# VectorE's first weight chunk and first v queued behind the first pair's copies, with that pair's k loaded from ScalarE's queue

## The chip, the cores and the metric

The kernel runs on one core of a Trainium2 chip. The metric is the device time of one execution in microseconds (us). The engines work side by side, each through its own instruction list in a fixed order: TensorE (PE, with its weight loads as PEld), VectorE (DVE), ScalarE (ACT), GpSimd (POOL) and SyncE (SP), which here does nothing but start transfers. ScalarE can start transfers too. An instruction that has to wait holds up everything behind it on its engine.

## What is computed

Attention over 4 batches of 8 heads, 576 positions and a head width of 64, in which only scores within tau of the row's maximum are kept; then two expert layers on the 2304 rows that come out.

```python
scores = scale * np.matmul(q, k.transpose(0, 1, 3, 2))
thresh = np.max(scores, axis=-1, keepdims=True) - tau
scores = np.where(scores >= thresh, scores, -1000000000.0)
attn = np.exp(scores - np.max(scores, axis=-1, keepdims=True))
x = np.matmul(attn / (np.sum(attn, axis=-1, keepdims=True) + 1e-09), v)
...
h = x @ w_in                        # first layer, 512 -> 2048
g = (a[0] + a[1]*h + a[2]*h**2 + a[3]*h**3) / (1.0 + abs(b[0])*abs(h) + abs(b[1])*h**2 + 1e-6)
x = g @ w_out                       # 2048 -> 512
...
h = x @ w_in                        # second layer, other weights
g = np.where(h >= 1.0, h, np.where(h <= -1.0, 0.0, (h + 1.0)**2 / 4.0))
out = g @ w_out
```

## The kernel before

All matrix products are made from pairs of 16-bit parts (a value and what is left of it), so every operand is scaled by a power of two and split into `hi` and `lo` first. For q and k that is `prep_pair`, which handles two heads (a pair) at a time: it loads q and k, squares them on ScalarE (L345) to bound them, finds the largest entry over all partitions with two TensorE products and a VectorE maximum (`everywhere`, L188, L189), makes a scale of it (`root`, L169 to L173), and splits (L215 and L216). For the first pair of the first batch, `turned` then transposes q and k with TensorE (L324) and copies the results out of PSUM: q by ScalarE (L328), k by VectorE (L330), and `kT2`, k with its two halves of the partitions exchanged, half by ScalarE (L331) and half by VectorE (L332). The other pairs are transposed by a transfer.

The weights arrive as 64-bit numbers. Each of the two layers has eight chunks, and each chunk two halves (`x` = 0 for w_in, 1 for w_out). `convert` loads a half of 1 MB into a tile `rw`, of which there are two, rebuilds 32-bit numbers in a tile `wt`, of which there are three, with three VectorE instructions (L229, L230, L231), bounds them (TensorE L254, VectorE L255, L189, L169 to L173), scales them on ScalarE (L218) and splits them (ScalarE L209, four GpSimd subtractions L213, which end the use of the `wt` tile). The first layer's halves stay on the chip as `wc`; the second layer's, `wh`, go back to memory.

The first batch's attention is a generator of its own, `first_attention`: pair 0 is prepared, v is loaded in ten pieces and bounded by VectorE (`first_v`, L510 to L522), pair 1 is prepared, and then for each of four pairs `row_max` finds the row maxima of the scores (TensorE L540 and L541, VectorE L544), which go into a row `mrow` (L580), and `transposed`, `sums`, `take` and `divide` do the rest, ending with the tiles `xT` (L633, L634). The next pair's `row_max` runs beside the current pair. After that come steps: 24 per layer and batch (three blocks of 192 rows by eight chunks), each a first product (L863), the function between (L744 to L757 in the first layer, L808 to L810 in the second) and a second product (L877). The attention of the next batch, 36 row tiles called softmax rows below (L442, L444, L404), runs beside those steps.

The order in which each engine gets its instructions is made when the kernel is built, by a scheduler that goes by priorities (`at`): a moved instruction may thus move many others. `tc.issue_after(ins)` makes the instructions of its block that run on the engine of `ins` stand behind `ins` in that engine's list; those on other engines are not bound. SP and ScalarE start transfers in the order of their lists.

Names in the rows: `wt_0_1` is chunk 0, half 1; `mqke` the bound of q and k; `qkr` their scale; `mv` the bound of v; `sm` and `mx` the scores and maxima of `row_max`.

Of the kernel before, what the change touches and what calls it, by code (L numbers as in the profile page):

```python
# [43 lines left out]
def tile_attention_moe_moe2(  # L44
# [18 lines left out]
    V, A, G, T, Q = nc.vector, nc.scalar, nc.gpsimd, nc.tensor, nc.sync  # L63
    B, H, S, D = q.shape
    P = 128
    NP = H // 2
    NT = S // P
    ST = S - NT * P
# [40 lines left out]
    def small(n, name, keep=False):  # L109
        if keep:  # L110
            return cp.tile([P, n], F32, name=name)
        tag = "".join(x for x in name if x.isalpha() or x == "_").rstrip("_")
        return sp.tile([P, n], F32, name=name, tag=f"s{n}_{tag}", bufs=4 if tag in ("mx", "nt") else 2)
# [62 lines left out]
    def at(when):  # L176

        return tc.high_priority(tc.cur_priority - int(1000 * (when + 100)))
# [83 lines left out]
    def make_half(m, i, x, wc, on_vector):  # L262
        convert(m, i, x, wc[:, x * HALF : (x + 1) * HALF], on_vector)
        if x == 1:
            with at(8 + i):
                Q.dma_start(scratch[m][i], wc)
# [20 lines left out]
    def whole(x):  # L287
        return x[..., 0 : NT * P, :].rearrange("h (p t) d -> p h (t d)", t=NT)

    def prep_v(b, on_vector=True):  # L290
# [24 lines left out]
                split(to[:, :, 0:D], to[:, :, D + 1 : 2 * D + 1], raw[:, n0:n1], s_x[b], on_vector)  # L315
        return vv

    def turned(qk, qT, kT, kT2):
        last = ps_1.tile([P, 512], F32, name="qk_t8", tag="ph1")
        for x in (1, 0):  # L320
            most = ps_2.tile([P, 1024], F32, name=f"qk_t{x}", tag="s" if x else "acc")
            for c in range(C):
                dst = most[:, c * P : (c + 1) * P] if c < C - 1 else last[:, x * P : (x + 1) * P]
                T.matmul(dst, qk[:, x, c], ident16, start=True, stop=True)  # L324
            for src, c0, c1 in ((most, 0, C - 1), (last[:, x * P : (x + 1) * P], C - 1, C)):
                src = src.rearrange("p (c s) -> p c s", s=P)
                if x == 0:
                    A.copy(qT[:, c0:c1], src)  # L328
                else:
                    V.tensor_copy(kT[:, c0:c1], src)  # L330
                    A.copy(kT2[0:D, c0:c1], src[D : 2 * D])  # L331
                    V.tensor_copy(kT2[D : 2 * D, c0:c1], src[0:D])  # L332

    def prep_pair(b, pr, on_vector=True):
        raws = rp.tile([P, 2, C + 1, D], F32, name=f"rqk{b}_{pr}", tag="rqk", bufs=1)
        raw = raws[:, :, 0:C, :]
        for x, src in enumerate((q, k)):
            Q.dma_start(raws[:, x].rearrange("p (a c) d -> p a (c d)", a=2)[:, :, 0 : NT * D],
                        whole(src[b, 2 * pr : 2 * pr + 2]))
            for ab in range(2):  # L340
                Q.dma_start(raw[ab * ST : (ab + 1) * ST, x, NT, :], src[b, 2 * pr + ab, NT * P :, :])
        mx = small(2, f"mqk{b}_{pr}")
        qk = ap.tile([P, 2, C, 2 * D], F16, name=f"qk{b}_{pr}", tag="qk", bufs=1)
        for x in range(2):
            A.activation(qk[:, x, :, 0:D], raw[:, x], AF.Square, scale=2.0**-32, accum_out=mx[:, x : x + 1])  # L345
        f = small(2, f"qkf{b}_{pr}")
        s = root(f"qkr{b}_{pr}", f, everywhere(f"mqke{b}_{pr}", mx, 2), 2.0**96, n=2)

        con = sp.tile([P, 4], F32, name=f"con{b}_{pr}", tag="con", bufs=3)
        V.scalar_tensor_tensor(con[:, 0:1], f[:, 0:1], cflag, f[:, 1:2], op0=ALU.mult, op1=ALU.mult)  # L350
        V.tensor_scalar(con[:, 1:2], con[:, 0:1], -1.0, None, op0=ALU.mult)
        V.scalar_tensor_tensor(con[:, 2:3], s[:, 0:1], tau8, s[:, 1:2], op0=ALU.mult, op1=ALU.mult)
        V.tensor_tensor(con[:, 2:3], con[:, 2:3], tlow, op=ALU.min)
        if b == 0:
            V.tensor_scalar(con[:, 3:4], con[:, 2:3], STEEP, -LARGEST, op0=ALU.mult, op1=ALU.max)
        for x in range(2):
            split(qk[:, x, :, 0:D], qk[:, x, :, D : 2 * D], raw[:, x], s[:, x : x + 1], on_vector)
        if b > 0 or pr < 2:
            qkT = ap.tile([P, 2 * C, P], F16, name=f"qkT{b}_{pr}", tag="qkT")
            qT, kT = qkT[:, 0:C], qkT[:, C : 2 * C]  # L360
            kT2 = ap.tile([P, C, P], F16, name=f"kT2{b}_{pr}", tag="kT2")
            if b == 0 and pr == 0:
                turned(qk, qT, kT, kT2)
                return con, qT, kT, kT2
            Q.dma_start_transpose(out=qkT, in_=qk.rearrange("p x c d -> p (x c d)"))
        else:
            qT, kT, kT2 = (ap.tile([P, C, P], F16, name=f"{x}{b}_{pr}", tag="eT" if pr == 2 else "hl", bufs=N_ROW)
                           for x in ("qT", "kT", "kT2"))
            for x, t in enumerate((qT, kT)):
                Q.dma_start_transpose(out=t, in_=qk[:, x].rearrange("p c d -> p (c d)"))  # L370
        Q.dma_start(kT2[0:D], kT[D : 2 * D])
        Q.dma_start(kT2[D : 2 * D], kT[0:D])
        return con, qT, kT, kT2
# [265 lines left out]
    def first_attention():  # L639

        pairs = [prep_pair(0, 0)]
        yield
        vv = first_v()
        xT[0] = [xp.tile([P, 2 * KT, TB], F16, name=f"xT0_{j}", tag="xT", bufs=NB) for j in range(NB)]
        mrows = [xp.tile([P, 1152], F16, name="mrow0", tag="yT", bufs=NB), mp.tile([P, 1152], F16, name="mrow1", tag="yo", bufs=1)]
        for t in mrows:
            G.memset(t, 0.0)
        yield
        pairs.append(prep_pair(0, 1, False))
        yield  # L650
        for _ in row_max(0, *pairs[0][1:], mrows[0]):
            yield
        n = 0
        for pr in range(NP):
            data = *pairs[pr], mrows[pr % 2]
            rows = row_max(pr + 1, *pairs[pr + 1][1:], mrows[(pr + 1) % 2]) if pr + 1 < NP else iter(())
            x = ap.tile([P, S], F32, name=f"x0_{pr}", tag="e", bufs=N_SC)
            d = ap.tile([P, S], F32, name=f"d0_{pr}", tag="sc", bufs=N_SC)
            held = []
            for ab, t in [(0, t) for t in range(NT + 1)] + [(1, t) for t in range(NT)]:  # L660
                e = transposed(pr, ab, t, data, n)
                for f in held:
                    f()
                if t == 0:
                    pv = [ps_1.tile([P, 512], F32, name=f"pv{z}_{pr}_{ab}", tag=tag)[:, 0 : S // 2]
                          for z, tag in enumerate(("pv", "ph1"))]
                    held = [partial(sums, pv, 1, pr, NT, tail, vv, True, False)] if ab else []
                    held.append(partial(sums, pv, ab, pr, t, e, vv, not ab, False))
                elif t == NT or (ab and t == NT - 1):
                    held = [partial(sums, pv, ab, pr, t, e, vv, False, True), partial(take, pv, ab, x, d)]  # L670
                    tail = e
                else:
                    held = [partial(sums, pv, ab, pr, t, e, vv, False, False)]
                for _ in range(2 if n % 9 < 6 else 1):
                    next(rows, None)
                n += 1
                yield
                if n in PREPARE:
                    pairs.append(prep_pair(0, len(pairs), False))
                    yield  # L680
            for f in held:
                f()
            divide(pr, x, d)
        yield
# [164 lines left out]
    chunks = {}  # L849
# [33 lines left out]
    steps = [(n, m, b, j, i) for n, (m, b) in enumerate(phases) for j in range(NB) for i in range(NCH)]  # L883

    att = first_attention()
    halves = [(i, x) for i in range(NCH) for x in range(2)]
    for i in range(NCH):
        chunks[0, i] = new_chunk(0, i)
    for n in range(N_FIRST):
        with at(36 * n / N_FIRST - 40):  # L890
            next(att)
        while halves and len(halves) * N_FIRST > 2 * NCH * (N_FIRST - 1 - n):
            with at(2.4 * (2 * NCH - len(halves)) - 39.5):
                i, x = halves.pop(0)
                make_half(0, i, x, chunks[0, i], False)


    beside = [[] for _ in steps]
# [79 lines left out]
```

## Time and profile before

| | |
|---|---|
| median of 3 runs | 1236.59 us (1235.79 to 1240.24) |
| the profiled execution | 1239.17 us, its span 1237.1 us |
| TensorE matmul / weight load busy | 1095.3 us (89%) / 988.4 us (80%) |
| VectorE busy | 979.3 us (79%) |
| ScalarE / GpSimd busy | 839.5 us (68%) / 542.7 us (44%) |
| moved by transfers | 175.51 MB, mean 142 GB/s |
| mean granted TensorE clock | 0.963 of full speed |

The busy shares are averages over stages with different limits: the start and the first attention, a stage in which the first layer runs beside the conversion of the second layer's weights, and a long stage of steps. The table by stages among the rows below separates them. "Idle before" in a row is the time in which that engine did nothing ahead of the instruction, with what ended it.

### The profile page before, as it was taken

How to read it: one execution, taken by the hardware profiler on the slowest of the kernel's cores; microseconds unless marked ns; L12 is line 12 of the kernel's file. 1: busy time of each engine (PE TensorE's matmuls, PEld its weight loads, DVE VectorE, ACT ScalarE, POOL GpSimd, SP SyncE). 2: the span in 40 equal slices, each digit the busy share in tenths (PEclk: the TensorE clock that was granted, in tenths of full speed). 3: DMA queues.
4: the chain of work that ended last, by engine and by line, in shares of the span. 5: the costliest groups of instructions: out<-in, count | busy, mean ns of one | idle time of the engine just before them, and what ended most of it. 6: DMA issues, size and time to landing. Idle time of an engine off the chain costs nothing.

```text
span 1237.1 us, 31750 instructions
## 1 busy us (share of the span) xinstructions
PE 1095.3 (89%) x12636; PEld 988.4 (80%) x12636; DVE 979.3 (79%) x2362; ACT 839.5 (68%) x1532; POOL 542.7 (44%) x698
## 2 busy tenths in 40 slices
PE   2778788588899999898888998998899999999998
PEld 1445456477888989898778888997888998999997
DVE  8887896999997377799997766899996768896431
ACT  2577777698887377677875766887675667775332
POOL 2445545656666266322564454223563553222221
PEclk9888888899899999999999999999999999999999
DMA  7677576635269158813785639422984467007000
GB/s 220 224 205 252 210 266 238 220 93 137 49 151 249 29 111 185 218 28 90 183 225 95 115 64 250 136 50 68 242 195 71 81 171 221 15 2 261 15 14 27
DMA packets 217845, 175.51 MB, mean 142 GB/s; under 512 B 179680, under 2 KB 190944, under 8 KB 209504
## 3 DMA queue, kind: packets, MB, share of 16 engines
q1 hardware_dynamic: 216464, 171.38, 52.6%
q8 instruction: 99, 1.62, 0.5%
q10 hardware_dynamic: 1232, 2.10, 0.5%
q14 instruction: 50, 0.41, 0.1%
HBM read 106.83 MB, written 21.50 MB: 104 GB/s over the span
## 4 chain that ended last, share of the span: by engine, by line
PE 40%; DVE 24%; DMA 11%; POOL 9%; issue 9%; ACT 6%; SPq 1%; DVEq 0%; ACTq 0%; POOLq 0%
PE acc L877 15%; PE ph L863 15%; DMA eT<-hl 8%; POOL hl L415 3%; PE pv L613 2%; PE pv L430 2%; DVE t L746 2%; POOL wh L213 2%; DVE e L404 2%; DVE t L751 2%; DVE sc L442 2%; POOL gg L213 1%; DVE t L757 1%; DVE t L748 1%; DVE t L747 1%
## 5 line engine op out<-in xcount | busy, mean ns | idle before, releaser
L877 PE MATMUL acc<-gg,wc 128*128 128x192 f16 x4608 | 427.6, 247 | 10.9 <-DVE mye L189 4.9
L863 PEld LDWEIGHTS <-wc 128*128 128x128 f16 x4608 | 388.9, 99 | 24.4 <-issue 16.5
L877 PEld LDWEIGHTS <-wc 128*128 128x128 f16 x4608 | 384.1, 98 | 12.6 <-issue 11.2
L213 POOL TENSOR_TENSOR gg<-t,gg 128x384 f16<-128x384 f32 x192 | 192.9, 1006 | 380.1 <-ACT gg L209 308.0
L863 PE MATMUL ph<-xT,wc 128*128 128x192 f16 x2304 | 218.1, 252 | 13.3 <-DVE t L748 13.2
L863 PE MATMUL ph<-yT,wc 128*128 128x192 f16 x2304 | 213.4, 246 | 3.7 <-DVE t L748 2.5
L415 POOL TENSOR_TENSOR hl<-e,hl 128x256 f16<-128x256 f32 x216 | 160.6, 764 | 0.0
L209 ACT CAST gg<-t 128x384 f16<-128x384 f32 x192 | 96.9, 508 | 75.1 <-DVE t L810 36.8
L809 DVE SCALAR_TENSOR_TENSOR t<-t,c 128x384 f32<-128x384 f32 x96 | 66.2, 690 | 88.9 <-ACT t L808 87.0
L404 DVE SCALAR_TENSOR_TENSOR e<-sc,nt,e 128x576 f32<-128x576 f32 x108 | 97.5, 903 | 28.1 <-ACT e L403 27.9
L413 POOL TENSOR_TENSOR hl<-e,hl 128x64 f16<-128x64 f32 x108 | 42.3, 391 | 147.7 <-ACT hl L412 134.0
L403 ACT ACTIVATE e<-sc,nt,con 128x576 f32<-128x576 f32 x108 | 93.3, 864 | 4.6 <-POOL hl L415 0.2
L808 ACT ACTIVATE t<-ph,c 128x384 f32<-128x384 f32 x96 | 63.9, 667 | 45.6 <-PE ph L863 45.3
L430 PE MATMUL pv<-v,eT 128*128 128x65 f16 (+3 forms) x1680 | 71.4, 195 | 25.2 <-DMA eT<-hl 24.1
L442 DVE TENSOR_SCALAR_CACHE_REDUCE sc<-s 128x576 f32<-128x576 f32 x108 | 80.8, 748 | 15.2 <-PE s L397 14.5
L412 ACT CAST hl<-e 128x576 f16<-128x576 f32 x108 | 72.1, 667 | 28.6 <-DVE e L404 28.0
L430 PEld LDWEIGHTS <-eT 128*128 128x128 f16 (+1 forms) x1680 | 64.0, 101 | 33.9 <-DMA eT<-hl 30.0
L744 ACT ACTIVATE t<-ph,sc 128x384 f32<-128x384 f32 x96 | 55.3, 576 | 50.6 <-PE ph L863 50.4
L213 POOL TENSOR_TENSOR wc<-wt,wc 128x256 f16<-128x256 f32 x64 | 55.1, 894 | 63.8 <-ACT wc L209 63.8
L749 ACT ACTIVATE t<-t,lc 128x384 f32<-128x384 f32 x96 | 67.8, 708 | 15.3 <-DVE t L746 14.9
L213 POOL TENSOR_TENSOR wh<-wt,wh 128x256 f16<-128x256 f32 x64 | 58.9, 950 | 35.8 <-ACT wh L209 35.7
L751 DVE SCALAR_TENSOR_TENSOR t<-t,ka,t 128x384 f32<-128x384 f32 x96 | 67.7, 705 | 8.7 <-ACT t L750 8.3
(238 smaller groups left out, 1910.9 us busy)
## 6 DMA issues: line engine op xcount, KB each, us to landing
wc<-scratch SPq DMA_DIRECT2D x56, 1024.0 KB, 5.9
rw<-in_moe_w_in_dram SPq DMA_DIRECT2D x15, 1024.0 KB, 5.7
rw<-in_moe_w_out_dram SPq DMA_DIRECT2D x15, 1024.0 KB, 5.4
scratch<-wc SPq DMA_DIRECT2D x8, 1024.0 KB, 4.5
scratch<-wh SPq DMA_DIRECT2D x16, 512.0 KB, 3.7
rqk<-in_q_dram SPq DMA_DIRECT2D x16, 256.0 KB, 3.1
rqk<-in_k_dram SPq DMA_DIRECT2D x16, 256.0 KB, 3.1
kT<-qkT SPq DMA_DIRECT2D x26, 144.0 KB, 2.5
```

Of the source, the lines that this page charges most:

```text
L209: A.copy(hi, src)
L213: G.tensor_tensor(lo[:, p], src[:, p], hi[:, p], op=ALU.subtract)
L403: A.activation(e, s, AF.Exp, bias=nb, scale=con[:, 0:1])
L404: V.scalar_tensor_tensor(e, s, th, e, op0=ALU.is_ge, op1=ALU.mult)
L412: A.copy(hi, e)
L415: G.tensor_tensor(lo_w[:, p], e[:, whole][:, p], hi[:, whole][:, p], op=ALU.subtract)
L430: T.matmul(pv[rows, 0:w], eT[:, c, cols], vv[:, h * NT + x if x < NT else H * NT + h, at : at + w], start=(n == 0), stop=(n == len(blocks) ...
L442: V.tensor_scalar(s, banks[:, 0:S], 1.0, -LARGEST, op0=ALU.mult, op1=ALU.max, accum_out=mx)
L749: A.activation(r, u, AF.Ln, bias=lc[:, 1:2], scale=lc[:, 0:1])
L751: V.scalar_tensor_tensor(s, s, ka[:, 0:1], r, op0=ALU.add, op1=ALU.mult)
L863: last = T.matmul(ph[:, f, :], w[:, wx, kt, f * P : (f + 1) * P], rhs, start=(n == 0), stop=(n == 3 * KT - 1))
L877: T.matmul(dst, w[:, wx, f, d * P : (d + 1) * P], gg[:, gx, f, :], start=(i == 0 and f == 0 and n == 0 and d % 2 == 0), stop=(i == NCH - 1 ...
```

## The change

It does three things. `turned` hands back its last VectorE copy (`done`), which is kept in `started`. The making of `first_v` and of both halves of chunk 0 of the first layer happens within `tc.issue_after(started[0])`, so all VectorE instructions of these stand behind that copy; their transfers and their work on other engines are not bound. And the first pair's k is loaded from ScalarE's queue, in one piece of 256 KB and two of 16 KB, where SP's queue loaded it before.

```diff
--- before.py
+++ after.py
@@ -315,6 +315,8 @@
                 split(to[:, :, 0:D], to[:, :, D + 1 : 2 * D + 1], raw[:, n0:n1], s_x[b], on_vector)
         return vv
 
+    started = []
+
     def turned(qk, qT, kT, kT2):
         last = ps_1.tile([P, 512], F32, name="qk_t8", tag="ph1")
         for x in (1, 0):
@@ -329,16 +331,18 @@
                 else:
                     V.tensor_copy(kT[:, c0:c1], src)
                     A.copy(kT2[0:D, c0:c1], src[D : 2 * D])
-                    V.tensor_copy(kT2[D : 2 * D, c0:c1], src[0:D])
+                    done = V.tensor_copy(kT2[D : 2 * D, c0:c1], src[0:D])
+        return done.ins
 
     def prep_pair(b, pr, on_vector=True):
         raws = rp.tile([P, 2, C + 1, D], F32, name=f"rqk{b}_{pr}", tag="rqk", bufs=1)
         raw = raws[:, :, 0:C, :]
         for x, src in enumerate((q, k)):
-            Q.dma_start(raws[:, x].rearrange("p (a c) d -> p a (c d)", a=2)[:, :, 0 : NT * D],
-                        whole(src[b, 2 * pr : 2 * pr + 2]))
+            queue = A if x and b == pr == 0 else Q
+            queue.dma_start(raws[:, x].rearrange("p (a c) d -> p a (c d)", a=2)[:, :, 0 : NT * D],
+                            whole(src[b, 2 * pr : 2 * pr + 2]))
             for ab in range(2):
-                Q.dma_start(raw[ab * ST : (ab + 1) * ST, x, NT, :], src[b, 2 * pr + ab, NT * P :, :])
+                queue.dma_start(raw[ab * ST : (ab + 1) * ST, x, NT, :], src[b, 2 * pr + ab, NT * P :, :])
         mx = small(2, f"mqk{b}_{pr}")
         qk = ap.tile([P, 2, C, 2 * D], F16, name=f"qk{b}_{pr}", tag="qk", bufs=1)
         for x in range(2):
@@ -360,7 +364,7 @@
             qT, kT = qkT[:, 0:C], qkT[:, C : 2 * C]
             kT2 = ap.tile([P, C, P], F16, name=f"kT2{b}_{pr}", tag="kT2")
             if b == 0 and pr == 0:
-                turned(qk, qT, kT, kT2)
+                started.append(turned(qk, qT, kT, kT2))
                 return con, qT, kT, kT2
             Q.dma_start_transpose(out=qkT, in_=qk.rearrange("p x c d -> p (x c d)"))
         else:
@@ -640,7 +644,8 @@
 
         pairs = [prep_pair(0, 0)]
         yield
-        vv = first_v()
+        with tc.issue_after(started[0]):
+            vv = first_v()
         xT[0] = [xp.tile([P, 2 * KT, TB], F16, name=f"xT0_{j}", tag="xT", bufs=NB) for j in range(NB)]
         mrows = [xp.tile([P, 1152], F16, name="mrow0", tag="yT", bufs=NB), mp.tile([P, 1152], F16, name="mrow1", tag="yo", bufs=1)]
         for t in mrows:
@@ -892,7 +897,8 @@
         while halves and len(halves) * N_FIRST > 2 * NCH * (N_FIRST - 1 - n):
             with at(2.4 * (2 * NCH - len(halves)) - 39.5):
                 i, x = halves.pop(0)
-                make_half(0, i, x, chunks[0, i], False)
+                with tc.issue_after(started[0]) if i == 0 else nullcontext():
+                    make_half(0, i, x, chunks[0, i], False)
 
 
     beside = [[] for _ in steps]
```

On VectorE's list, right behind the instructions on the small constants (the last is L154), stood before the rebuilding of chunk 0 and the first bound of v, with pair 0's bound `mqke` and scale `qkf` among them:

```order
L229 TENSOR_SCALAR wt_0_0_218<-rw_0_0_216 128x1024
L230 SCALAR_TENSOR_TENSOR wt_0_0_218<-rw_0_0_216,wt_0_0_218 128x1024
L231 SCALAR_TENSOR_TENSOR wt_0_0_218<-rw_0_0_216,wt_0_0_218 128x1024
L229 TENSOR_SCALAR wt_0_1_334<-rw_0_1_332 128x1024
L230 SCALAR_TENSOR_TENSOR wt_0_1_334<-rw_0_1_332,wt_0_1_334 128x1024
L516 TENSOR_REDUCE mv_249<-v_246 128x1
L189 TENSOR_REDUCE mqke_0_166<-pmmqke_0_167 128x2
L231 SCALAR_TENSOR_TENSOR wt_0_1_334<-rw_0_1_332,wt_0_1_334 128x1024
L516 TENSOR_REDUCE mv_249<-v_246 128x1
L169 TENSOR_SCALAR qkf_0_165<-mqke_0_166 128x2
L255 TENSOR_REDUCE gram<-pg_0_0_222 128x1
L516 TENSOR_REDUCE mv_249<-v_246 128x1
```

Now that place holds pair 0's bound, scale and constants, and then its split, its copies out of PSUM, and only then chunk 0 and v (L332 and L334 are the copies that were L330 and L332):

```order
L216 SCALAR_TENSOR_TENSOR qk_0_162<-rqk_0_154,qkr_0_s,qk_0_162 128x9x64 x2
L332 CAST qkT_0_185<-qk_t_188 128x1024
L332 CAST qkT_0_185<-qk_t_187 128x128
L334 CAST kT_0_186<-qk_t_188 64x1024
L334 CAST kT_0_186<-qk_t_187 64x128
L229 TENSOR_SCALAR wt_0_0_218<-rw_0_0_216 128x1024
L520 TENSOR_REDUCE mv_249<-v_246 128x1 x3
L229 TENSOR_SCALAR wt_0_1_334<-rw_0_1_332 128x1024
L520 TENSOR_REDUCE mv_249<-v_0_247 128x1
L524 TENSOR_REDUCE mv_249<-v_1_248 64x1 x2
L548 TENSOR_REDUCE mx_0_327<-sm_00_328 128x1
L230 SCALAR_TENSOR_TENSOR wt_0_0_218<-rw_0_0_216,wt_0_0_218 128x1024
```

Pair 0's copies, which stood at rows 51 to 56 of the list, stand at rows 29 to 32; the three rebuilding steps of each half of chunk 0 have moved from rows 19 to 26 to rows 33 to 46, among the maxima `mx` of pair 0, and v's bounds go with them.

On ScalarE's list, from the load of `b_t` on, before:

```order
L120 DMA b_t<-in_moe_b_dram 128x2
L242 DMA rw_0_0_216<-in_moe_w_in_dram 128x4x512
L345 ACTIVATE qk_0_162,mqk_0_161<-rqk_0_154 128x9x64
L242 DMA rw_0_1_332<-in_moe_w_out_dram 128x2x1024
L151 ACTIVATE lc<-lc 128x1
L345 ACTIVATE qk_0_162,mqk_0_161<-rqk_0_154 128x9x64
L215 ACTIVATE qk_0_162<-rqk_0_154,qkr_0_s 128x9x64 x2
```

and now:

```order
L120 DMA b_t<-in_moe_b_dram 128x2
L342 DMA rqk_0_154<-in_k_dram 128x2x256
L345 DMA rqk_0_154<-in_k_dram 64x64
L151 ACTIVATE lc<-lc 128x1
L345 DMA rqk_0_154<-in_k_dram 64x64
L349 ACTIVATE qk_0_162,mqk_0_161<-rqk_0_154 128x9x64
L242 DMA rw_0_0_216<-in_moe_w_in_dram 128x4x512
L349 ACTIVATE qk_0_162,mqk_0_161<-rqk_0_154 128x9x64
L242 DMA rw_0_1_332<-in_moe_w_out_dram 128x2x1024
L215 ACTIVATE qk_0_162<-rqk_0_154,qkr_0_s 128x9x64 x2
```

The load of chunk 0's first half, which was the fourth transfer of the list, now comes behind the first activation on q (L349 now, L345 before); the third piece of k stands behind the logarithm L151, which needs VectorE's result L149.

On SP's list, from the first load of q on, before:

```order
L338 DMA rqk_0_154<-in_q_dram 128x2x256
L341 DMA rqk_0_154<-in_q_dram 64x64 x2
L338 DMA rqk_0_154<-in_k_dram 128x2x256
L341 DMA rqk_0_154<-in_k_dram 64x64 x2
L510 DMA v_246<-in_v_dram 128x4x64 x6
L510 DMA v_0_247<-in_v_dram 128x4x64 x2
L512 DMA v_1_248<-in_v_dram 64x4x64 x2
L242 DMA rw_1_0_376<-in_moe_w_in_dram 128x4x512
L242 DMA rw_1_1_418<-in_moe_w_out_dram 128x2x1024
L338 DMA rqk_1_289<-in_q_dram 128x2x256
L341 DMA rqk_1_289<-in_q_dram 64x64 x2
L338 DMA rqk_1_289<-in_k_dram 128x2x256
L341 DMA rqk_1_289<-in_k_dram 64x64 x2
```

and now:

```order
L342 DMA rqk_0_154<-in_q_dram 128x2x256
L345 DMA rqk_0_154<-in_q_dram 64x64 x2
L514 DMA v_246<-in_v_dram 128x4x64 x6
L514 DMA v_0_247<-in_v_dram 128x4x64 x2
L516 DMA v_1_248<-in_v_dram 64x4x64 x2
L342 DMA rqk_1_289<-in_q_dram 128x2x256
L345 DMA rqk_1_289<-in_q_dram 64x64 x2
L342 DMA rqk_1_289<-in_k_dram 128x2x256
L345 DMA rqk_1_289<-in_k_dram 64x64 x2
L242 DMA rw_1_0_376<-in_moe_w_in_dram 128x4x512
L242 DMA rw_1_1_418<-in_moe_w_out_dram 128x2x1024
L242 DMA rw_2_0_507<-in_moe_w_in_dram 128x4x512
```

Without k, v follows q at once. The loads of pair 1 (`rqk_1`), which share one tile with pair 0's, now stand ahead of those of chunk 1 (`rw_1_0`, `rw_1_1`), which stood ahead of them before.

## Rows read from the trace of the kernel before

**Rows 1.** Busy time by stage: stretch, length, busy per engine (instructions), clock, transfers.
```profile
core 0: us, PE busy (x) PEld busy (x) DVE busy (x) ACT busy (x) POOL busy (x), PEclk, DMA share, GB/s
...
7.80:20.30 12.50, 3.37 (x14) 2.33 (x14) 9.60 (x17) 0.84 (x3) 0.00 (x0) 1.00 0.88 251
...
60.00:229.00 169.00, 136.21 (x840) 88.43 (x839) 137.38 (x301) 125.48 (x196) 86.73 (x98) 0.84 0.69 233
229.00:375.00 146.00, 122.18 (x1380) 112.52 (x1380) 142.11 (x334) 125.60 (x235) 95.76 (x108) 0.93 0.49 129
375.00:550.00 175.00, 166.84 (x2171) 159.44 (x2170) 123.93 (x309) 114.06 (x220) 77.16 (x106) 0.99 0.58 135
```

**Rows 2.** Chain of waits within the first 250 us, its shares by line.
```profile
by line: PE pv L613 11.3%; issue 7.9%; POOL wh L213 7.7%; POOL wc L213 5.8%; DVE wt L231 5.3%; DVE wt L230 5.2%; DVE mx L544 4.8%; DVE wt L229 4.5%; ACT wt L218 3.5%; DMA rw<-in_moe_w_out_dram 2.7%; DMA rw<-in_moe_w_in_dram 2.6%; PE st L598
```

**Rows 3.** Timeline, pair 0's k and bound: start, us, engine, line, operation, idle before.
```profile
2.50 0.59 SPq L338 DMA_DIRECT2D rqk<-in_k_dram  x1
...
4.47 2.44 SPq L341 DMA_DIRECT2D rqk<-in_k_dram  x2
...
7.10 0.15 DVE L149 TENSOR_SCALAR lc<-babs 128x1 f32<-128x1 f32 x1
...
10.41 0.68 ACT L345 ACTIVATE qk<-rqk 128x576 f16<-128x576 f32 x1 [2.65 <-DMA rqk<-in_k_dram]
...
11.24 0.79 PE L188 MATMUL pmmqke<-ident,mqk 128*128 128x128 f32 x2 [2.66 <-ACT qk L345]
```

**Rows 4.** Timeline of VectorE, pair 0's chain: bound, scale, split, copies.
```profile
16.28 0.41 DVE L189 TENSOR_REDUCE mqke<-pmmqke 128x2 f32<-128x256 f32 x1
...
19.99 0.15 DVE L173 RECIPROCAL qkr_s<-qkf 128x2 f32<-128x2 f32 x1
...
22.45 0.81 DVE L216 SCALAR_TENSOR_TENSOR qk<-rqk,qkr_s,qk 128x576 f16<-128x576 f32 x1
...
25.40 1.42 DVE L330 CAST qkT<-qk_t 128x1024 f16<-128x1024 f32 x2
...
28.52 1.42 DVE L332 CAST kT<-qk_t 64x1024 f16<-64x1024 f32 x2
```

**Rows 5.** Timeline of TensorE, the transposes of pair 0's k.
```profile
23.75 1.17 PE L324 MATMUL qk_t<-fixed,qk 128*128 128x128 f16 x9
```

**Rows 6.** Timeline of VectorE: chunk 0, first half, and one bound of v.
```profile
10.01 0.69 DVE L229 TENSOR_SCALAR wt<-rw 128x1024 int32<-128x1024 int32 x1 [2.22 <-DMA rw<-in_moe_w_in_dram]
...
12.00 1.23 DVE L231 SCALAR_TENSOR_TENSOR wt<-rw,wt 128x1024 int32<-128x1024 int32 x1
...
15.68 0.68 DVE L516 TENSOR_REDUCE mv<-v 128x1 f32<-128x512 f32 x1
```

**Rows 7.** Timeline of SP: the loads of chunk 1's first half and of chunk 2's.
```profile
17.16 0.53 SPq L242 DMA_DIRECT2D rw<-in_moe_w_in_dram  x1
...
28.46 0.37 SPq L242 DMA_DIRECT2D rw<-in_moe_w_in_dram  x1
```

**Rows 8.** Transfers by line: number, KB each, median us from issue to landing.
```profile
rw<-in_moe_w_in_dram SPq DMA_DIRECT2D x15, 1024.0 KB, 5.7
...
rw<-in_moe_w_in_dram ACTq DMA_DIRECT2D x1, 1024.0 KB, 7.8
...
rqk<-in_k_dram SPq DMA_DIRECT2D x32, 16.0 KB, 2.5
```

**Rows 9.** Groups of VectorE from 229 to 400 us: busy us, mean ns, idle before.
```profile
L404 DVE SCALAR_TENSOR_TENSOR e<-sc,nt,e 128x576 f32<-128x576 f32 x18 | 18.1, 1005 | 0.0
...
L442 DVE TENSOR_SCALAR_CACHE_REDUCE sc<-s 128x576 f32<-128x576 f32 x18 | 13.4, 745 | 1.2 <-PE s L397 1.2
```

**Rows 10.** Groups of TensorE from 229 to 400 us, the same columns.
```profile
L396 PE MATMUL s<-qkT 128*128 128x512 f16 (+3 forms) x40 | 10.4, 288 | 2.2 <-DVE sc L442 1.6 <-DMA qkT<-qk 0.7
L430 PE MATMUL pv<-v,eT 128*128 128x65 f16 (+1 forms) x196 | 9.5, 194 | 1.8 <-DVE fy L825 1.0 <-DMA eT<-hl 0.8
L397 PE MATMUL s<-kT,qkT 128*128 128x512 f16 (+3 forms) x40 | 8.1, 286 | 0.0
```

## The prediction

> **What bounds the kernel now.** I read the busy time by stage first, to see which engine limits what, then the chain of waits of the start, then the timeline of the two chains that the change touches. From 229 to 375 us VectorE is the limit: 142.11 of 146 us busy. From 375 to 550 us TensorE takes over with 166.84 of 175, and VectorE has some 51 us to spare. Before 229 us nothing is full: VectorE is busy for 137.38 of the 169 us from 60 to 229, the most of all engines, and still 31.6 us idle [rows 1]. The chain of waits there runs through both jobs of that stage, the weights (L229 to L231, L218, the GpSimd subtractions, the loads) and the attention of batch 0 (L613, L544, L598), with no line over 11.3% [rows 2]. So the start is limited by VectorE together with hand-overs between engines, and the change reorders VectorE's list in it.
>
> What the change aims at is visible. Pair 0's bound was ready for VectorE at 11.24 + 0.79 = 12.03 us [rows 3], but VectorE took it up at 16.28. Its scale ended at 20.14, its second split at 23.26, and the copies of k out of PSUM at 25.40 to 29.94 [rows 4]. In between VectorE did chunk 0 and v [rows 6].
>
> **Part 1: k from ScalarE's queue.** Before, k's three pieces were issued by SP from 2.50 to 6.91 us, and the activation that waited for them started at 10.41 [rows 3]. On ScalarE's new list two pieces go out early, but the third stands behind the logarithm L151, which needs VectorE's L149, done at 7.25 [rows 3]. With that activation and one issue of about 0.59 us the third piece leaves at about 8.0; a piece of 16 KB takes 2.5 us [rows 8], so k is complete at about 10.5. Bounds: were nothing in its way, three issues of 0.59 from about 2.2 would end near 4.0, some 2.9 us ahead of 6.91, and the whole chain would gain as much; were the landing as slow as before (10.41 - 6.91 = 3.5 us), it would lose 1.1. I take nothing, since the place of the third piece in the list decides. The Trainium skill speaks against this part too (DMA: Bandwidth & Descriptors, section "Issuing engines are not separate DMA queues"): transfers begun from different engines share the same 16 DMA engines, and a second issuer saves only the time of issuing. By that rule the part is worth at most the issue time, and by the rows it is worth nothing; the 2.9 us above are such issue time, so no run here yet shows the rule wrong. SP, freed of k, issues v sooner, but nothing on VectorE asks for v before 20 us now, so that is worth nothing either.
>
> **Part 2: pair 0 first.** With k at 10.4 the bound is ready at 12.03 as before, and VectorE now takes it at once: 0.41 for the maximum, 0.15 each for three steps of the scale, so the scale ends at about 12.95 instead of 20.14. One ScalarE pass over the tile (0.68, taken from L345 over the same tile [rows 3]) and two splits of 0.81 end at about 15.3 [rows 4]. TensorE's transposes of k began 0.49 after the second split (23.75 - 23.26) and took 1.17 [rows 5]: they end at about 17.0. The copies, 1.42 and 1.42 [rows 4], end at about 19.9, **10.0 us earlier** than 29.94. That is the whole gain on offer.
>
> **What it costs.** VectorE now waits where it worked. Between 7.8 us and 19.9 us it has 0.41 + 0.45 + five small ones of about 0.15 (0.75) + 1.62 + 2.84 = 6.1 us of work; chunk 0 fills the 0.4 us to 20.3. Before, it did 9.60 us in that stretch [rows 1]. So by 20.3 it has done **3.1 us** less.
>
> Then chunk 0 and v come, mixed with pair 0's maxima. Up to L231 of chunk 0's first half the list holds two L229 (0.69), two L230 (1.23, as L231), one L231, four full v bounds and two of half size (0.68 and about 0.4), and three maxima (as wide as a v bound, 0.68): 1.4 + 2.5 + 1.2 + 3.5 + 2.0 = 10.6 us [rows 6], so it ends at about 30.5. Only then is a tile `rw` free, and SP can issue the load of chunk 1's first half, which it issued at 17.16 before [rows 7]: **13.3 us later**. On SP that load has also pair 1's loads ahead of it, but those wait only for the splits at 15.3. The load takes 5.7 us in the median, 7.8 where two ran together [rows 8]: it lands at 36.2 (38.3). VectorE gets there after four maxima, one L231 and two small maxima, 4.6 us, at 35.1. So it waits **1.1 us**, between nothing and 3.2; I take 1.1, from the median, because only one other load is near it. The next `wt` tile has to be given back by GpSimd; that wait exists before and after, so I put no difference on it. Who waits for VectorE: pair 1's scale stands at about the same place of the list, so it comes later by the same 4 us, and with it pair 1's split and transposes.
>
> The sum of part 2 on VectorE is 3.1 + 1.1 = **4.2 us of work later** from 36 us on. If that stays until 375 us, with the stage from 229 on full, all of it is lost time. Its bounds are wide: it can be made up among the 31.6 us of idle time before 229 us (then pair 0's lead of 10.0 counts), or grow; both ends are rivals below.
>
> **Part 3: what the scheduler moves further on.** Counted in the two lists of VectorE, 17 softmax rows of batch 1 stood ahead of the maximum that ends the third block of the first layer, and now 10 do; by the maximum that ends the first block of batch 1's first layer the two lists hold the same again. So 7 rows go from the VectorE-bound stage into the TensorE-bound one. They take 7 x (1.005 + 0.745) = 12.3 us of VectorE's work along [rows 9]. Of TensorE's they take 14 of the 40 instructions each of L396 and L397 (14 x 18.5 / 40 = 6.5 us) and 71 x 9.5 / 196 = 3.4 us of L430: 9.9 us [rows 10], which must be done later, where TensorE is the limit. Net 9.9 - 12.3 = **-2.4 us**. Its other bound is nothing, if TensorE already sets the end of that stage; I take -2.4, as VectorE is 97% busy there [rows 1].
>
> **The sum:** +4.2 - 2.4 = +1.8 us. On the profiled execution, 1239.17 us (its span is 1237.1), that is 1241.0. That execution lies 2.6 us above the median of the three runs, so on the median, 1236.59, the forecast is **1238.4 us**. A measurement of this kernel can tell about 0.5%, 6.2 us, from no change: faster begins below 1230.4, slower above 1242.8. The forecast is no change.
>
> **Rival A, faster: the attention's chain is the limit of the start.** Then VectorE's lost 4 us vanish in its idle time, and pair 0's lead of 10.0 us travels through four pairs to the first step. For it: pair 0's chain stood idle from 12.03 to 16.28 waiting for VectorE alone, attention lines have the largest share of the chain, and 31.6 us of idle time can take up 4.2. Against it: `mrow` needs VectorE's maxima, which now stand mixed with chunk 0, and pair 1's scale comes later, not sooner. Price: 1236.59 - 10.0 = **1226.6 us**; it is a measurable gain once over 6.2 of the 10.0 us come through.
>
> **Rival B, slower: the train of weight loads is the limit.** With two `rw` tiles each load waits for a VectorE step, so a first load that leaves 13.3 us later moves all 32 halves of both layers, whose last halves are converted beside the first steps. Place: the L229 of each half, waiting for its load or for GpSimd. For it: conversion lines fill much of the chain of waits, GpSimd's weight subtractions alone 7.7% + 5.8% [rows 2], and 28.46, the load of chunk 2, becomes about 42. Against it: VectorE can run conversions closer together, since its list has fewer maxima left then. Price: 13.3 - 2.4 = +10.9, **1247.5 us**; it decides from 8.6 of the 13.3 us on.
>
> **Rival C: the order holds, but no time changes hands.** Waiting of 4.2 us is taken up before 229 us and pair 0's lead too. Then only part 3 is left: 1236.59 - 2.4 = 1234.2 us. It lies within no change and shares its chance with the forecast.
>
> **How the numbers follow.** The forecast and C together get 45 in 100, of which the forecast has 28; A 27, B 28. A and B are close because each stands on one of the two chains that the waits show mixed. The range reaches to both rivals' full prices, 1226 to 1248, and what is left out is an effect beyond them. Faster 0.27, same 0.45, slower 0.28.
>
> **What the profile after would show.** Part 1: the activation on k starts within 1 us of 10.41. Part 2: the second copy of k ends near 20 us, SP's first load of chunk 1 leaves near 30.5, and L229 of chunk 1 waits for it about 1 us. If the first `xT` of pair 3 comes 6 us or more sooner, A is right; if VectorE's L229 waits add up to some 8 us more before 229 us, B is. Part 3: from 229 to 375 us VectorE stays full and the softmax rows in it are fewer, and from 375 on TensorE stays above 95%. I am wrong if VectorE's idle time before 60 us does not grow by about 4 us, or if the returned rows come too late for batch 1's first step and TensorE idles there.

## The result and the profile after

The changed kernel takes 1245.67 us (median of 13 runs, 1242.36 to 1251.48) where the kernel before, run beside it, takes 1238.47 us (13 runs, 1235.23 to 1245.12). The ratio is 1.0063, with a 95% interval of 1.0044 to 1.0083: **slower by 0.63%, 7.8 us by the ratio** (the two medians lie 7.2 us apart). The forecast was no change, +1.8 us. The range held the time, but by the text's own mark of 0.5% this is a loss. The profiled execution of the changed kernel took 1251.48 us, the longest of its 13 runs, so differences between the two profiled executions are larger than those of the medians. Below, a reading counts only if it comes back in the profiles of other kernels.

**The start went as planned.** VectorE's timeline after, pair 0's chain, then chunk 0, the first step of chunk 1, and `mrow` (start, us, engine, line, operation, idle before):

```profile
10.99 0.42 DVE L189 TENSOR_REDUCE mqke<-pmmqke 128x2 f32<-128x256 f32 x1 [3.84 <-PE pmmqke L188]
...
12.92 1.55 DVE L216 SCALAR_TENSOR_TENSOR qk<-rqk,qkr_s,qk 128x576 f16<-128x576 f32 x2 [0.27 <-DMA v<-in_v_dram]
15.72 1.42 DVE L332 CAST qkT<-qk_t 128x1024 f16<-128x1024 f32 x2 [1.25 <-PE qk_t L326]
18.02 1.42 DVE L334 CAST kT<-qk_t 64x1024 f16<-64x1024 f32 x2 [0.88 <-ACT kT L333]
...
28.20 1.21 DVE L231 SCALAR_TENSOR_TENSOR wt<-rw,wt 128x1024 int32<-128x1024 int32 x1
...
34.95 0.69 DVE L229 TENSOR_SCALAR wt<-rw 128x1024 int32<-128x1024 int32 x1 [1.21 <-DMA rw<-in_moe_w_in_dram]
...
43.98 0.68 DVE L584 CAST mrow<-pmr 3x512 f16<-3x512 f32 x1
```

The copies that ended at 29.94 [rows 4] end at 19.44 us. L229 of chunk 1 comes at 34.95 and waits 1.21 us for its load. But `mrow`, the next thing that all of pair 0 waits for, comes at 43.98, against 44.55 in the same view of the kernel before:

```profile
44.55 0.68 DVE L580 CAST mrow<-pmr 3x512 f16<-3x512 f32 x1
...
91.46 0.41 DVE L634 SCALAR_TENSOR_TENSOR xT<-x,v_s,xT 128x192 f16<-128x192 f32 x1
...
228.85 0.85 DVE L634 SCALAR_TENSOR_TENSOR xT<-x,v_s,xT 128x192 f16<-128x192 f32 x1 [0.19 <-ACT xT L633]
```

and after:

```profile
91.31 0.41 DVE L638 SCALAR_TENSOR_TENSOR xT<-x,v_s,xT 128x192 f16<-128x192 f32 x1
...
233.86 0.74 DVE L638 SCALAR_TENSOR_TENSOR xT<-x,v_s,xT 128x192 f16<-128x192 f32 x2
```

A lead of 10.5 us at the copies is 0.6 us at `mrow` and 0.15 us at pair 0's first `xT` (91.46 to 91.31): the maxima ahead of `mrow` stand among chunk 0's steps on VectorE, and by the lists, whichever goes first, `mrow` needs all the maxima. By pair 3's `xT` the changed kernel is 5.0 us behind. That comes back: in four kernels whose VectorE has the list of before up to there, pair 3's first `xT` starts at 225.0 to 228.9 us, and in the three that have the change's list up to there at 229.7 to 233.9.

**The stages after, beside [rows 1].** The same four stretches:

```profile
7.80:20.30 12.50, 5.14 (x25) 3.34 (x26) 6.75 (x17) 4.64 (x9) 0.00 (x0) 1.00 0.89 274
60.00:229.00 169.00, 130.62 (x837) 85.11 (x834) 142.29 (x309) 127.63 (x198) 88.02 (x103) 0.89 0.76 252
229.00:375.00 146.00, 120.94 (x1325) 113.48 (x1326) 139.20 (x310) 119.24 (x223) 97.33 (x100) 0.90 0.44 126
375.00:550.00 175.00, 161.32 (x2108) 150.53 (x2107) 124.87 (x316) 115.27 (x217) 70.67 (x110) 0.97 0.61 137
```

By 20.3 us VectorE has done 9.60 - 6.75 = 2.9 us less. By 60 us it lacks more, 51.67 - 44.84 = 6.8 us. The first 60 us, before and then after:

```profile
0.00:60.00 60.00, 29.26 (x174) 18.13 (x175) 51.67 (x121) 25.84 (x41) 21.73 (x37) 0.96 0.70 220
0.00:60.00 60.00, 32.10 (x180) 19.63 (x180) 44.84 (x112) 24.54 (x39) 16.05 (x33) 0.91 0.57 171
```

From 60 to 229 us VectorE does 142.29 - 137.38 = 4.9 us more: its idle time there takes work up, and 1.9 us are still missing at 229. From 375 on TensorE is busy for 161.32 of 175 us (92%) where it was 166.84; the prediction expected over 95%.

The border between the two limits lies better at the third block's maximum (L189 writing `mye`, 395.3 us before, 386.3 after). These are the stretches from pair 3's `xT` to it, and from it to batch 1's first such maximum. Before, then after:

```profile
228.80:395.30 166.50, 140.81 (x1612) 130.57 (x1613) 157.32 (x369) 139.32 (x264) 109.73 (x126) 0.94 0.57 150
395.30:559.10 163.80, 156.69 (x2031) 149.58 (x2031) 117.91 (x298) 107.61 (x204) 64.31 (x89) 0.99 0.50 113
```

```profile
233.90:386.30 152.40, 129.96 (x1465) 123.01 (x1464) 144.19 (x320) 122.84 (x229) 96.19 (x99) 0.92 0.44 125
386.30:568.80 182.50, 168.06 (x2165) 157.09 (x2165) 133.47 (x335) 124.15 (x234) 71.33 (x110) 0.97 0.56 122
```

The first stretch is 14.1 us shorter, with 13.1 us less of VectorE's work. The second is 18.7 us longer, with 11.4 us more of TensorE's work and 7.3 us more in which TensorE idles (163.80 - 156.69 = 7.1, and 182.50 - 168.06 = 14.4). What the idle time waits for, from the table of waits of TensorE in that second stretch (us in all, times, longest), before and after:

```profile
PE pv L430 <- DMA eT<-hl: 5.3, 5, 2.2
```

```profile
PE pv L434 <- DMA eT<-hl: 12.7, 9, 4.7
```

`eT` is a softmax row that SP's queue transposes on its way; L434 (L430 before) reads it. The longest of these waits, in the timelines of SP and then TensorE after:

```profile
381.91 0.53 SPq L278 DMA_DIRECT2D wc<-scratch  x1
...
385.90 0.53 SPq L278 DMA_DIRECT2D wc<-scratch  x1
386.54 5.01 SPq L421 DMA_TRANSPOSE eT<-hl  x1
```

```profile
390.25 2.14 PE L882 MATMUL acc<-gg,wc 128*128 128x192 f16 x24
397.07 0.94 PE L434 MATMUL pv<-v,eT 128*128 128x65 f16 x14 [4.68 <-DMA eT<-hl]
```

The transposing transfer was issued behind two 1 MB loads of second-layer weights (and smaller loads between them), its issue alone took 5.01 us, and its reader started 10.5 us after the issue began. TensorE came to that reader 4.68 us too early, and the steps' products behind it on its list stood still with it.

### The profile page after: what moved, and what is told of

It is laid out like the page before. It is cut to its first block, busy times and chain, and to the rows that moved or that the text cites. A ratio compares the mean times of both kernels' runs of the same rounds, so it can differ in the third digit from the quotient of the medians.

```text
span 1249.7 us, 31764 instructions
## 1 busy us (share of the span) xinstructions
PE 1095.7 (88%) x12636; PEld 986.9 (79%) x12636; DVE 985.8 (79%) x2362; ACT 842.5 (67%) x1532; POOL 534.3 (43%) x698
## 4 chain that ended last, share of the span: by engine, by line
PE 36%; DVE 19%; DMA 10%; issue 7%; POOL 6%; ACT 4%; SPq 1%; DVEq 0%; POOLq 0%; ACTq 0%
PE ph L868 16%; PE acc L882 16%; DMA eT<-hl 8%; POOL hl L419 3%; PE pv L434 2%; DVE t L751 2%; DVE t L756 2%; DVE e L408 2%; POOL gg L213 1%; DVE t L762 1%; DVE t L753 1%; DVE t L752 1%; DVE sc L446 1%; POOL hl L417 1%; ACT hl L416 1%
## 5 line engine op out<-in xcount | busy, mean ns | idle before, releaser
L868 PE MATMUL ph<-yT,wc 128*128 128x192 f16 x2304 | 217.7, 248 | 5.0 <-DVE rk_f L160 1.8
L419 POOL TENSOR_TENSOR hl<-e,hl 128x256 f16<-128x256 f32 x216 | 155.9, 741 | 0.0
L434 PE MATMUL pv<-v,eT 128*128 128x65 f16 (+3 forms) x1680 | 70.9, 194 | 37.9 <-DMA eT<-hl 37.7
L434 PEld LDWEIGHTS <-eT 128*128 128x128 f16 (+1 forms) x1680 | 62.8, 101 | 47.4 <-DMA eT<-hl 45.2
L756 DVE SCALAR_TENSOR_TENSOR t<-t,ka,t 128x384 f32<-128x384 f32 x96 | 68.5, 714 | 11.2 <-ACT t L755 10.8
```

The costliest lines, as they stand in the source:

```text
L419: G.tensor_tensor(lo_w[:, p], e[:, whole][:, p], hi[:, whole][:, p], op=ALU.subtract)
L434: T.matmul(pv[rows, 0:w], eT[:, c, cols], vv[:, h * NT + x if x < NT else H * NT + h, at : at + w], start=(n == 0), stop=(n == len(blocks) ...
L756: V.scalar_tensor_tensor(s, s, ka[:, 0:1], r, op0=ALU.add, op1=ALU.mult)
L868: last = T.matmul(ph[:, f, :], w[:, wx, kt, f * P : (f + 1) * P], rhs, start=(n == 0), stop=(n == 3 * KT - 1))
```

## The experiments

Two theories. **Later order:** the start costs little, and the loss comes from the order that the scheduler gives the instructions far behind the edit, above all the softmax rows of batch 1. **Start:** the loss comes from the lost VectorE time and the late loads before 60 us. Every ratio below is against the kernel before, run beside it on the same chip. The runs stand on several chips, so ratios can be compared with each other, and medians in us cannot.

### Moving the softmax rows alone

Three kernels move batch 1's softmax rows by the table that spreads them over the steps. On the kernel before:

```diff
-ATTENTION = {1: (18, 50), 2: (60, 100), 3: (108, 147)}
+ATTENTION = {1: (16, 50), 2: (60, 100), 3: (108, 147)}
```

> The kernel before, with one number changed: batch 1's attention is spread from step 16 instead of 18. VectorE's list is the same as before for its first 416 rows (up to the last pair's xT), but only 10 softmax rows stand ahead of the maximum of the third block, as in the changed kernel (17 before). If the change lost its time by where the later rows stand: slower than before by 0.4 to 0.8%, with TensorE waiting longer for eT between 386 and 570 us. If the delay at the start is what is lost: same as before within 0.3%.

Measured: 1243.40 us, ratio 1.0045 (1.0024 to 1.0065). VectorE's list is that of before for its first 416 instructions, and 10 rows instead of 17 stand ahead of the third block's maximum, as in the change. With an untouched start, some two thirds of the loss appear, and TensorE waits 7.9 us for `eT` from the third block's maximum to batch 1's first, where it waited 5.3 before.

With `(14, 50)` in that place 21 rows stand ahead:

> The kernel before with batch 1's attention spread from step 14: the start as before, 21 softmax rows ahead of the third block's maximum instead of 17. If the place of the rows decides: 0 to 0.4% faster than before. If the start decides: same as before within 0.3%.

Measured: 1240.48 us, 1.0029 (1.0005 to 1.0052). A miss for the first theory: more rows early is not faster, and the 0.3% that the other allowed just holds. And the change with `(14, 50)`, which brings back 20 rows:

> The changed kernel with batch 1's attention spread from step 14: the start of the change (list the same for 401 rows), but 20 softmax rows ahead of the third block's maximum instead of 10. If the place of the rows decides: back to the time before, ratio 0.997 to 1.002. If the delay at the start decides: as slow as the change, ratio 1.004 to 1.008.

Measured: 1248.36 us, 1.0098 (1.0068 to 1.0128). Another miss, for both theories. So the number of rows ahead is not the law by itself, and neither is the wait for `eT`. With 21 rows ahead, from pair 3's `xT` to the third block's maximum, then to batch 1's first, and TensorE's largest wait in the first of these stretches and its wait for `eT` in the second:

```profile
230.00:404.60 174.60, 145.94 (x1620) 133.49 (x1620) 163.36 (x376) 142.12 (x269) 111.20 (x127) 0.92 0.52 142
404.60:563.00 158.40, 153.86 (x2019) 147.45 (x2018) 113.89 (x282) 104.21 (x197) 60.85 (x86) 1.00 0.53 116
PE s L396 <- DVE sc L442: 9.1, 9, 2.0
PE pv L430 <- DMA eT<-hl: 2.8, 4, 1.0
```

The second stretch and its wait for `eT` are shorter than before (163.8 and 5.3 us), but the first is longer by more (174.6 against 166.5). So here time is lost in another stage and by another wait. All the same, these three kernels and the change, whose lists all came out anew, are slower than the kernel before, by 0.3% to 1.0%. An edit that lets the scheduler make a new list can't tell the two theories apart; the order has to be held.

### Without ScalarE's queue

```diff
-            queue = A if x and b == pr == 0 else Q
+            queue = Q
```

> The change without its second part: k goes through SyncE's queue as before, chunk 0 and v still stand behind pair 0's copies. 8 softmax rows stand ahead of the third block's maximum. Both theories: slower than before by 0.4 to 1.0%. What it tells is the price of k's way: if ScalarE's queue is worth nothing, the second copy of k ends within 1 us of the 19.44 us of the changed kernel; if it is worth its issue time, 2 to 3 us later.

Measured: 1251.72 us, 1.0125 (1.0094 to 1.0157). In the profile, the second copy of k and the activation that waits for k:

```profile
10.39 0.68 ACT L349 ACTIVATE qk<-rqk 128x576 f16<-128x576 f32 x1 [2.57 <-DMA rqk<-in_k_dram]
```

```profile
19.08 1.41 DVE L334 CAST kT<-qk_t 64x1024 f16<-64x1024 f32 x2 [0.88 <-ACT kT L333]
```

The copies end at 20.5 us instead of 19.4, so ScalarE's queue is worth 1.1 us on that chain, between the two marks of the expectation. The ratio lies above the expected 0.4 to 1.0%, and again mixes this with a new later order (8 rows ahead instead of 10). Here that order loses its time earlier than in the change: pair 0's first `xT` comes at 91.74 us, but pair 3's 11.4 us after the one of before (228.85):

```profile
240.25 2.25 DVE L638 SCALAR_TENSOR_TENSOR xT<-x,v_s,xT 128x192 f16<-128x192 f32 x3
```

### The order held

From here on, each kernel carries a table of one of the two lists from some point on, and binds TensorE, VectorE, ScalarE and GpSimd to it. The bonds are of order of issue only and add no wait; SP's list stays the scheduler's.

```diff
+        for x, y in [(x, ranks[0]) for x in sorted(first)] + list(zip(ranks, ranks[1:])):
+            tc.add_manual_dep(own[name][y], own[name][x].name,
+                              mybir.DependencyInfo(mybir.DependencyClass.NoSync, mybir.DependencyReason.DATA), reason="order")
...
     while pending:
         with at(st + 1.5):
             finish_step()
+    keep_order(tc, nc)
```

First the change's start with the order of before from about 91 us on (VectorE's instruction 184), and the reverse, the start of before with the change's order from there:

> The changed kernel, in which VectorE, TensorE, ScalarE and GpSimd are held to the order of the kernel before from VectorE's 184th instruction group on (about the first pair's xT, 91 us); the start keeps the change's order. The start alone, without what the scheduler moved later. If the loss lies in the later order: same as before, ratio 0.998 to 1.002, and the first xT near 91 us. If the delay at the start is carried to the end: 1.003 to 1.007.

> The kernel before, with the start as it was, and held to the changed kernel's order from about 91 us on. The later order alone. If the loss lies in the later order: 1.004 to 1.008, as the change. If the start decides: same as before, 0.998 to 1.002.

Measured: the start alone 1237.75 us, 1.0015 (0.9991 to 1.0039); the later order alone 1245.92 us, 1.0071 (1.0046 to 1.0096). The start has its effect (copies end at 19.8 us) and its time can't be told from no change. The later order, behind a start that was not touched, is as slow as the change.

Then the two parts of the start, each with the later order of before: k on ScalarE's queue without the queueing, and the queueing with k on SP's queue.

```diff
-        with tc.issue_after(started[0]):
-            vv = first_v()
+        vv = first_v()
```

> Only k's load from ScalarE's queue, without the queueing behind pair 0's copies, and the order of the kernel before held from about 91 us on. If the start is worth nothing: same as before, 0.998 to 1.002; the copies of k end between the 19.4 us of the change and the 29.9 us of before, and chunk 0's rebuilding fills the gaps of pair 0's chain, so VectorE idles less before 30 us than in the change.

> Only the queueing of chunk 0 and v behind pair 0's copies, with k from SyncE's queue, and the order of the kernel before held from about 91 us on. If the start is worth nothing: same as before, 0.998 to 1.002. If the start's delay is carried on, at least as slow as the kernel with both parts and the held order, by up to the 1 us by which k is later.

Measured: k alone 1240.90 us, 1.0027 (1.0001 to 1.0052), copies at 22.7 us, with VectorE idle for 5.2 us of the first 30 where the change has 8.2; the queueing alone 1239.26 us, 1.0025 (1.0003 to 1.0048), copies at 20.4 us. Neither is faster. Both lie above the expected 0.998 to 1.002, and their intervals leave out no change by a hair: the start gains nothing, and may cost some 0.2%.

### Where in the later order

Four more kernels cut the order at pair 3's `xT` (about 229 us; VectorE's instruction 430 before, 441 after) and at batch 1's first maximum (about 560 us; 1041 and 1036). From about instruction 1420 on the two lists of VectorE are the same in any case.

> The change's own order of issue on TensorE, VectorE, ScalarE and GpSimd up to about 229 us (start and first stage), and from there the order of the kernel before. Theory (the loss comes from the stages after 229 us, where softmax rows of batch 1 and their reads now stand among the weight steps): no change against before, ratio 0.998 to 1.003, and the third block's maximum to batch 1's first within 2 us of the 163.8 us of the kernel before. Rival (the loss comes from the order between 91 and 229 us, which brings pair 3's xT 5 us later): ratio 1.004 to 1.009, with pair 3's xT near 234 us and no catching up after it.

> The order of issue of the kernel before, its start too, up to about 229 us, and the change's own order from there on. Theory (loss after 229 us): ratio 1.004 to 1.009, pair 3's xT near 229 us as before, TensorE's idle time that ends on a transposed eT tile 35 us or more over the run (24.1 before). Rival (loss between 91 and 229 us): ratio 0.998 to 1.003.

> The change's own order of issue on TensorE, VectorE, ScalarE and GpSimd up to batch 1's first maximum (569 us in the profile after), and from there the order of the kernel before. Theory (the loss comes from the stage between 229 us and there, where batch 1's softmax rows and their reads stand among the weight steps): ratio 1.004 to 1.009, as for the change. Rival (the loss comes from the order of the second and third layers, 570 to about 780 us, after which VectorE's list is the same in both kernels): ratio 1.000 to 1.003.

> The order of issue of the kernel before, its start too, up to batch 1's first maximum (559 us in the profile before), and from there the change's own order. Theory (loss between 229 us and there): ratio 0.998 to 1.003. Rival (loss from the order after it): ratio 1.004 to 1.009.

| the change's order stands | ratio | 95% interval | us by median |
|---|---|---|---|
| to 91 us | 1.0015 | 0.9991 to 1.0039 | 1237.75 |
| to 229 us | 1.0020 | 1.0000 to 1.0039 | 1239.24 |
| to 570 us | 1.0065 | 1.0039 to 1.0091 | 1243.71 |
| throughout (the change) | 1.0063 | 1.0044 to 1.0083 | 1245.67 |
| from 91 us | 1.0071 | 1.0046 to 1.0096 | 1245.92 |
| from 229 us | 1.0071 | 1.0045 to 1.0098 | 1242.98 |
| from 570 us | 0.9984 | 0.9958 to 1.0011 | 1234.77 |

Read from above and from below, the step of the ratio lies between 229 and 570 us; other steps are too small to be told from nothing. The theory's ratios held for all four kernels, the rival's for none. One number of the theory failed: TensorE's wait for `eT` over the whole run is 30.2 us with the order from 229 us on, not 35 or more, and 30.9 us with the order up to 229 us, so the sum over the run does not separate them. Within the stage it does. None of the four beats the kernel before by more than can be measured; the last comes nearest.

With the change's order up to 570 us, the two stretches and TensorE's wait for `eT` in the second:

```profile
232.80:383.10 150.30, 128.78 (x1465) 122.24 (x1464) 142.88 (x321) 122.61 (x229) 97.43 (x99) 0.94 0.47 126
383.10:560.70 177.60, 165.39 (x2165) 155.11 (x2165) 133.63 (x336) 124.38 (x234) 71.65 (x110) 0.99 0.56 126
```

```profile
PE pv L558 <- DMA eT<-hl: 11.2, 9, 3.5
```

With the change's order only from 570 us on:

```profile
225.00:389.80 164.80, 140.67 (x1599) 130.05 (x1600) 157.35 (x368) 138.83 (x263) 108.53 (x126) 0.94 0.56 151
389.80:551.20 161.40, 155.98 (x2050) 149.06 (x2047) 118.10 (x298) 108.01 (x205) 64.17 (x89) 1.00 0.52 116
```

```profile
PE pv L555 <- DMA eT<-hl: 4.5, 5, 1.5
```

Eight profiles can be sorted so, four with the order of before in that stage (the kernel before, the start alone, to 229, from 570) and four with the change's (the change, from 91, from 229, to 570). In us:

| | order of before | the change's order |
|---|---|---|
| first stretch | 166.5, 164.1, 162.7, 164.8 | 152.4, 150.0, 158.3, 150.3 |
| second stretch | 163.8, 162.4, 161.9, 161.4 | 182.5, 178.3, 176.9, 177.6 |
| TensorE busy in the second | 156.7, 155.0, 155.2, 156.0 | 168.1, 165.9, 165.8, 165.4 |
| wait for `eT` in the second | 5.3, 6.0, 4.9, 4.5 | 12.7, 10.6, 10.1, 11.2 |

No row overlaps, and the profiles of the two kernels with one part of the start and the order of before lie within the left column or at most 0.3 us outside it. The granted clock does not explain the rows: with the change's order up to 570 us it is 0.94 and 0.99 in the two stretches, as before. By the means of four, the first stretch is 11.8 us shorter (164.53 to 152.75) and the second 16.4 us longer (162.38 to 178.82). Of that, 10.6 us are work that came in (155.7 to 166.3) and about 6 us the longer wait for `eT` (5.2 to 11.1). Net +4.7 us of the 7.8. The lengths of both stretches together do overlap (324.6 to 330.3 us against 327.9 to 335.2), but TensorE's idle time in them does not (29.5 to 32.8 us against 33.7 to 36.9). The step of the ratio, from 1.0020 to 1.0065, is 5.6 us, with an error of some 4 us.

What stays open: that the wait for `eT` is what makes the difference is read from these traces. Moving the readers later on TensorE's list, or `eT` earlier on SP's, was not tried. SP's list was not held, so the runs do not part the engines' order from the order of the transfers that goes with it.

## Why the prediction was right and wrong

That the range held the time is luck as to the cause: its upper end is the price of rival B, and B is not what happened. The forecast's own sum, +1.8 us, missed a loss of 7.8.

**Part 1, worth nothing: off by 1.1 us on the chain, right for the time.** The third piece of k left sooner than the 8.0 us of the text, and the activation on k started at 9.33, not 10.41 [rows 3]. ScalarE's timeline after:

```profile
6.65 0.49 ACTq L345 DMA_DIRECT2D rqk<-in_k_dram  x1
...
9.33 0.68 ACT L349 ACTIVATE qk<-rqk 128x576 f16<-128x576 f32 x1 [1.29 <-issue]
```

With k on SP it started at 10.39 (above). So 1.06 us were saved, where SP's issues of k had taken 0.59 + 2.44 = 3.03 us [rows 3]. The Trainium skill (DMA: Bandwidth & Descriptors, section "Issuing engines are not separate DMA queues") says that a second issuer saves the time of issuing and no more. The trace agrees: less than the issue time was saved.

**Part 2, the start: the mechanism right to within some 1.1 us up to 35 us.** Predicted copies 19.9, measured 19.44, in which two errors offset each other: with k on SP's queue, where k comes as early as the text took it to come, they end at 20.4 to 20.5, and ScalarE's queue gives 1.1 us back; VectorE's missing work by 20.3 us 3.1, measured 2.9; chunk 0's L231 at 30.5, measured 29.41; chunk 1's L229 at 35.1 after 1.1 us of waiting, measured 34.95 and 1.21. SP's timeline after has the load of chunk 1 at 29.44 us, forecast for 30.5, against 17.16 [rows 7]:

```profile
29.44 0.37 SPq L242 DMA_DIRECT2D rw<-in_moe_w_in_dram  x1
```

**Part 2's carry, +4.2 us to the end, was probably too large.** The start alone measured 0.15%, 1.9 us (-1.1 to 4.8), so 4.2 lies inside but the best value is under half of it. The lag itself came: VectorE lacked 6.8 us of work at 60 us, and pair 3's `xT` came 5.0 us late. But VectorE lacked only 1.9 us at 229, for it had done 4.9 us more from 60 on. The text knew of 31.6 us of idle time there and gave the recovery to its rivals.

**Part 3, -2.4 us, is the step that failed.** The rows moved as counted; the groups of VectorE between pair 3's `xT` and the third block's maximum hold 17 of them before (first line) and 10 after:

```profile
L404 DVE SCALAR_TENSOR_TENSOR e<-sc,nt,e 128x576 f32<-128x576 f32 x17 | 17.3, 1016 | 0.0
...
L408 DVE SCALAR_TENSOR_TENSOR e<-sc,nt,e 128x576 f32<-128x576 f32 x10 | 9.4, 937 | 0.0
...
L446 DVE TENSOR_SCALAR_CACHE_REDUCE sc<-s 128x576 f32<-128x576 f32 x10 | 7.4, 744 | 0.9 <-PE s L401 0.9
```

Its two terms came out too: -12.3 of VectorE's work became 11.8 us off the first stretch, +9.9 of TensorE's became +10.6 in the second (the text's 71 instructions of L430 are 84 by the views: 196 before, 112 after). What was missing is a third term, which the text put at nothing: each moved row also brings a read of a transposed tile into the list of the engine that is now the limit. TensorE idles there for 12.5 us in the mean of four where it idled for 6.7, and waits for `eT` for 11.1 where it waited for 5.2. That is about +6 us, and the sum of part 3 is +4.7 instead of -2.4. The place of the term is shown by the held orders; that it is the wait for `eT` is read from the traces. The prediction named something near it as a sign that it is wrong ("the returned rows come too late for batch 1's first step and TensorE idles there") and gave it no price.

**Rival A** (1226.6) is wrong: the lead of 10 us is all but gone at `mrow`, and pair 3's `xT` comes later, not sooner. **Rival B** (1247.5) came close in time for another reason: up to 229 us VectorE's L229 waits for loads 3.7 us in all after (1.2 and 2.5) against 4.3 before (3.7 and 0.6), not 8 us more, though the loads of chunks 1 and 2 leave 12.3 and 11.1 us later (29.44 and 39.52 us), and the start alone can't be told from no change. **Rival C**'s first half, that the start's waits are taken up, is nearest to what the runs show.

## What to carry to other kernels

Where a scheduler makes the lists, a local edit is two changes: the edit, and a new order everywhere behind it. Hold the later order by bonds that add no wait and time the halves apart; here the edit alone gained nothing (1.0015, 0.9991 to 1.0039) and the order alone cost 0.7%. And when work moves from a stage with one limit to a stage with another, price the waits for its transferred tiles as well as its busy time: on the engine that limits the stage, 6 us more of such waits went with 6 us more of idle time here.

## What was not expected of the hardware

- A transposing transfer issued right behind two loads of 1 MB took 5.01 us to issue and 10.5 us to its reader's start, against a median of 3.7 us from issue to landing over all 108 transfers of `eT` in that execution. It came back with the same order in another kernel (the order up to 570 us): 3.20 us to issue, 9.3 us to landing, 3.5 us of TensorE's time. But it is not the order's own: in the kernel before one that was issued at 370.02 us landed 10.9 us later, and there all of TensorE's waits for `eT` in the stage that VectorE limits come to 0.8 us [rows 10]. Here a late transfer cost by where its reader stood.
- Order is worth a lot: the change and the twelve kernels above do the same work, apart from the queue that loads one pair's k, and their ratios spread over 1.4% (0.9984 to 1.0125), more than twice the effect under study.
